# Turning q and k of two batches with DMA transposes instead of TensorE, in a fused attention and FFT-gate kernel, with its schedule planned anew

## The chip, the cores and the metric

The kernel runs on one core of one Trainium2 chip. The metric is the time of one execution on the device in microseconds (us); three runs of the kernel before took 175.73, 176.09 and 177.28 us, median 176.09.

## The reference

Four batches, eight heads, 768 positions, head size 64. Attention sees the first eight keys (global) and the last 96 (local), with a bias for distance. Its output is projected to three parts; the middle one is convolved over the sequence through an FFT, multiplied with the other two, and projected again. Inputs and output are float32.

```python
# attention: q, k, v are (4, 8, 768, 64)
scores = (q @ k.T) / 8 + bias          # -slope * distance, slopes 2**-(h+1)
keep = (pos_k < 8) | ((rel >= 0) & (rel < 96))
a = softmax(where(keep, scores, -1e9))
x = (a @ v)                             # to (4, 768, 512)
# gate
x1, x2, x3 = split(x @ w_proj, 3)       # w_proj is (512, 1536)
conv = irfft(rfft(x2, axis=1) * rfft(filter_fft, axis=0))
out = (x1 * conv * x3) @ w_out          # (4, 768, 512)
```

## The kernel before

**Engines and names.** TensorE (PE) does the matmuls and transposes, ScalarE (ACT) and VectorE (DVE) copy the results from PSUM banks to SBUF and do the elementwise work, GpSimd (POOL) issues the loads, and SyncE (SP) issues the stores and a few small copies. POOL's loads read float32 from HBM and write fp16 into SBUF: they cast on the way.

**Attention, `attention(b)`.** For each batch the rows of q go to `qn` (six tiles of 128 rows), those of k to `kn` and of v to `vn` (seven tiles of 120 rows each, below eight rows that hold the global keys). `qn` and `kn` exist once, so a load of the next batch waits until the tile there was read; `vn` exists twice. A matmul of the scores needs q and k with the head dimension on the partitions. For batches 1 to 3 the method `transposes` does this for one tile: four PE transposes of 128x128, each with two heads, into one PSUM bank (line 938), then one copy on ACT or DVE to `QT` or `KT` (line 567). After k tile 0, a DVE copy spreads the eight global columns in `KT` over all seven tiles. `QT` and `KT` exist once as well. Batch 0 comes in pairs of heads in another layout (`load_pair`, `transpose_pair`, line 630): pair 0 is loaded as float32 by SP and cast by ACT or DVE, pairs 1 to 3 are cast by POOL's loads.

The tiles come in three groups, `GRP = [(0, 1), (2, 3), (4, 5, 6)]`. For each group and each pair of heads `scores` does the matmuls (line 975), ACT the exponentials (line 990), DVE the mask (line 997); `values` does the second matmul (lines 1015 and 1020), DVE divides by the sum (line 1039), and `transpose_x` turns the result into `xT` (line 1060).

**Gate and convolution.** `gate` projects `xT` to the first and third part (line 1098); `butterfly` and `conv(b)` do the middle part: projection (line 1159), forward transform (line 924), products with the filter's spectrum on DVE, inverse transform (lines 1181 and 1184), and in `project` the last matmul (line 1215), a copy to `ot` and the store by SP. The filter's spectrum is made in the kernel too.

**The order.** The program is first written down as a graph of operations (`Plan.op`), each with its engine or choice of engines, a cost in us, what it reads and writes, and the PSUM banks it takes. `lay` then goes through the graph like a list scheduler: among the operations that can start first on their engine, it takes the one with the lowest rank. A rank is the operation's batch and place in it plus a number from the list `NUDGES` (2112 numbers, two for each operation: one for the rank, one for the choice between ACT and DVE). `FAVOUR` is a constant in that choice. DMAs have a cost for the issue, and a cost for each packet on the DMA engines, which SP's and POOL's share. Each engine then runs its list in order. `fill` puts idle matmuls (line 563) where PE would wait long. Attention of batch b+1 is so mixed with the convolution of batch b.

Of the kernel before, what the change touches and what calls it, by code (L numbers as in the profile page):

```python
# [17 lines left out]
NG = 8  # L18
# [46 lines left out]
class Plan:  # L65
# [90 lines left out]
    def lay(self):  # L156
# [84 lines left out]
        830, 19469, 28342, 22698, -36791, 44557, 0, 38863, 17326, 50370, 0, 17086, -14969, 46246, -10719,  # L241
        3803, 22479, 12714, -995, -27474, -4380, 3973, 17122, 3529, 7380, -663, -24781, -3497, 45666, -4551,
        -35801, 10005, 0, 12791, 0, -10379, 0, 45454, 0, -5437, 0, -14061, -19757, -14504, -37905, -18946,
        0, -32477, 0, -19819, 0, 19446, -1510, 8329, 0, 27319, 11852, 7297, -33522, -3329, -24534, -36612,
        -27852, 3113, -7029, -29691, -14381, -3884, 31147, 32034, 41013, 3882, -7384, -6372, -2549, 6629,
        68912, 8963, -61766, 5547, -44599, 12091, 18399, 14042, 6929, -4982, -7955, 13539, -24252, 20179,
        -37287, 999, -15997, -18090, 9312, 22827, 23386, 28496, -25966, 23940, -7783, 39729, 0, 1069, 0,
        12644, 0, -10150, 0, 23681, 0, -18062, 0, -19460, 0, 7837, 0, 430, 0, -3637, 0, 8913, 0, -4969, 0,
        4698, 0, 6387, -28901, -14115, 14320, -44762, 8724, -14864, 46735, -14488, 23611, -14772, -11847,
        6451, -3306, -18377, -60, 4689, 27298, 24083, -497, -18877, 16900, 19934, 37256, 19651, -14734,  # L250
        -9560, 12718, -42257, 27146, 1115, -39200, -14114, 6946, -5667, 16361, -49626, -3804, -7768, -67026,
        -18259, 60927, 21512, -46061, 5299, 29871, 21514, -44548, 5866, -12730, -23878, -15725, 33821,
        20215, -25471, 41707, 6771, 23796, 39844, 27531, -14231, -2302, -5026, 6456, 8053, 1663, -7662,
        -1658, -22536, 10581, -5577, -28542, -40863, -38468, -5794, -5468, 40622, -19008, 14370, 67736,
        -58861, 42786, 25155, -29878, -3418, 3618, 4708, -22659, -28259, -20518, 8701, 6031, -6892, -10351,
        -20996, 26804, 20150, 54288, -13311, 5794, 6136, 52867, -15428, -29665, 25192, 30956, 45334, 21269,
        43306, 2557, -24451, 6157, -1880, -4325, -2390, 7965, -31500, -28218, 18854, 4142, 15094, -27249,
        27912, 43510, -17851, -24582, -28451, 3289, -4573, 52435, 13404, 20792, -24567, 15357, -28602,
        -63577, -4124, -16002, 20822, -14047, -23587, 29959, -35143, 9243, -7310, -76644, -8134, 42347,
        15822, -12242, -3646, -30686, 275, 21750, -36005, 1469, 29713, -50088, -42560, -19350, 23864, 5050,  # L260
        -35144, 35778, -23119, -25177, 16491, -2020, 4380, -36451, -22654, -22150, -20473, 13426, -26733,
        26609, 6268, -22149, 3957, -50217, -3909, -19153, 2810, -3292, 7853, -21492, 32509, 30392, 1058,
        -3422, 15580, -35441, -9203, -35466, 64502, 42951, -19116, -24283, 2677, -62640, -12510, -59703,
        11602, 21513, 35378, 20196, 11922, -1695, 2261, 5554, -11981, 15156, 12890, -23779, -19040, -49831,
        -15466, -43761, 7442, 2473, -11475, -562, -20186, 44257, -33302, -12882, -28759, 38437, 11482, 1330,
        11240, -38355, 17055, 27903, 51476, 19276, 41100, -22953, 19243, -49765, 30962, -35331, 10963,
        42827, 51939, -23434, -11212, 50785, -4094, -27838, -30215, -24532, -12422, 67855, 13805, 3349,
        -31574, -50206, -1578, -23241, 3462, -29661, 8300, 12759, 26155, 16907, 2610, 5092, 33120, -6934,
        14181, -6832, 37905, -14123, 4017, -27020, -20812, 1598, 3482, -15360, 14795, 14629, 485, 23373,
        31416, -26303, 985, -32770, -12960, -31274, -27569, 14995, 28878, -62352, -24591, -25434, -13467,  # L270
        -1753, 33337, -31036, -11856, -18317, -11803, -33535, -27683, -51311, -11621, 1840, -23345, -13880,
        -10610, -21888, -29421, -35794, 9291, 16111, -10016, -61858, 13788, 28430, 11863, 10235, 26016,
        -11573, 27177, -20634, 32822, -31295, 24126, 16224, 34719, 32835, 36139, 40036, 830, 39163, 18794,
        23592, 7759, 51877, 15207, 11097, 5209, -31196, 47785, 18050, 12543, -18408, 3112, 9419, 28821,
        33481, 24315, -4637, -2954, 58662, 10982, 44569, -17852, -13026, 18502, 18480, 661, 39608, 43043,
        5607, -6149, 51251, -23733, 21791, 22094, 13091, 28673, -13130, 38566, 29894, 58869, 14114, 22687,
        13217, 23944, 14851, 18542, 32490, 39556, 0, 2287, 0, 19051, 0, -4358, 0, -11746, 0, 19030, -37967,
        1328, 0, -1449, 14563, -17652, -982, -19950, 0, -1349, 0, -11190, 0, 2329, 0, 1474, 0, 9498, 0,
        18549, 0, 6688, 0, 22215, 0, 20539, 0, 3845, 0, 18493, 0, -9540, 0, 5625, 0, -4323, 0, -8046, -3533,
        -19460, 16225, 5133, -15664, 1868, -10430, 13679, -822, -6032, 46722, 17, -12126, -14344, -697,  # L280
        -13742, -12505, 35119, 19976, 12563, -17553, -4315, -16313, -8060, -26919, -13513, 5645, -9234,
        -8261, 33619, 1834, -2859, -2550, 21273, 8957, -13081, -9314, 20868, 8922, -5132, 5559, 6221,
        -35799, 24500, 3519, -6685, 3949, -816, -6213, 9623, -62952, -17310, 10679, 22559, -35498, 10601,
        -12029, 6157, 5514, 7375, -48803, 10526, -28598, 4222, -27669, -30984, 26626, 10987, -54583, -53116,
        -15825, 15071, -78852, -9661, 6714, 2840, -38629, -19587, -4267, 24678, -95876, 18875, -65326,
        37035, -57223, 2718, -80355, 8544, -25562, 24290, -40863, 2118, -56826, 1618, -8022, -31710, 24818,
        3620, -25827, 27844, -44889, 2870, 4692, 1799, -40217, -9884, -31044, -26859, 10139, -30260, 15490,
        -10550, -33083, -6484, -3536, 42406, -39070, 25617, -4598, 29316, -41708, 15965, 36737, 22936,
        -38817, 8527, -48993, 22443, 17760, 28836, -35248, -5369, -32024, 12970, -29506, 46391, 21693,
        -7287, -24248, -581, -2018, 24139, -49992, 23604, -37246, -19201, -50818, 32705, -650, -7523, -9491,  # L290
        -6925, -30680, 1857, -10661, 4404, 11499, 32387, -17435, -48594, -14949, -4657, -84287, -8566,
        14498, -17867, 2527, 39846, -8706, -27278, 52664, 6571, -35366, -320, -10331, -13919, -41255,
        -14510, -27402, 30994, -7841, -31169, -15489, 10258, -20175, 13543, 2857, 2578, 131, -1314, -20053,
        -3100, 4481, -24160, -39099, 11687, -27948, -9199, -2494, 30419, -9029, -805, -6822, -33325, 13405,
        -16820, -66296, -481, -11964, 10636, -6248, -15247, -30087, 9838, -10144, -26515, -24439, -29855,
        -22320, -23621, -44190, -16823, -1332, 20402, -52166, -32146, 29136, -8657, -32420, -27767, 19595,
        4945, -41783, -6152, 22710, -839, 24762, 12982, -46639, 45086, -32249, -27885, 26993, 32349, -1139,
        -27028, 5428, -35713, -11537, -21816, 4520, 11355, -11306, -17012, 4480, -2042, -15007, 18089,
        16310, 5551, -12842, -12327, -74283, -24015, -51377, 27730, -6713, 30891, -54126, 34332, -19745,
        -18476, -68884, 4160, 17961, -25458, -47047, -23408, -74718, -25716, -25378, 10363, -21807, -25577,  # L300
        -30760, -512, -35125, -15528, 5905, 11983, -39028, 8438, -56403, -744, -68035, -9455, -28679, 15786,
        -55653, 8176, -11569, -5453, 4461, 21051, 30451, 38894, -23961, -22340, -37283, -19384, -14914, 91,
        -24447, -19426, -32077, 21216, 6861, -6808, -6892, 5217, 10775, -14628, 70698, 20491, 17063, -9496,
        43779, -27379, 19441, -35221, 40472, -6558, 6850, 27498, 19585, 24533, 14892, -3738, -53050, 27975,
        -49714, -29727, 2330, -4593, -32440, 10709, 5615, -11179, -8091, 16512, -42979, 22940, -7459,
        -19376, -58359, -5155, 3527, 14869, 75937, 14885, 50802, -44287, 9855, -3550, 31325, 23170, 11445,
# [1108 lines left out]
```

## Time and profile before

| | |
|---|---|
| three runs | 175.73, 176.09, 177.28 us; median 176.09 |
| the profiled execution | 177.28 us, span in the profile 175.5 us |
| granted PE clock, mean over the span | 0.996 of full |
| PE | 166.9 us busy, 95% of the span, 1768 matmuls |
| DVE | 157.0 us, 89% |
| ACT | 152.6 us, 87% |
| POOL | 75.3 us, 43%, all of it before 99 us |
| transposes of whole tiles, line 938 | 156 matmuls, 219 to 220 ns each, first at 38.1 us, last at 111.7 |
| scores of batch 2 | first at about 72 us, last at 104 |
| scores of batch 3 | first at about 117 us, last at 134 |

The span is the profiled execution's time on the engines; its own time has the start and end around it as well. The busy time of PE counts each matmul from start to end; since they are pipelined, one may take 219 ns and the next start after 56. In the lists of groups, a line says which engine ran which operation, what it wrote from what, the shape and the number, then busy time, the mean of one in ns, and how long the engine sat idle just before, with what ended the wait. In the chain, each row is a start, a length and what ran.

### The profile page before, as it was taken

The page shows a single profiled execution, that of the slowest core. Times are in us where ns is not written, and L with a number is a line of the kernel's source. Part 1 is how long each engine was busy: PE and PEld are TensorE (multiplying, and loading weights), DVE is VectorE, ACT ScalarE, POOL GpSimd, SP SyncE. Part 2 cuts the span into 40 slices and gives each one's busy share as a digit, 9 for nine tenths or more (in the row PEclk, how much of TensorE's full clock was granted, in tenths as well). Part 3 has the DMA queues.
Part 4 walks back from the last instruction along what each step waited for, and adds up shares of the span by engine and source line. Part 5 has one row for each costly group of instructions (what it writes and reads, how often), then busy time and mean ns, then how long its engine had stood idle before and what let it go on. Part 6 is the DMA issues. An engine that isn't in the chain of part 4 may idle for free.

```text
span 175.5 us, 4566 instructions
## 1 busy us (share of the span) xinstructions
PE 166.9 (95%) x1768; PEld 104.3 (59%) x1768; DVE 157.0 (89%) x368; ACT 152.6 (87%) x304; POOL 75.3 (43%) x97
## 2 busy tenths in 40 slices
PE   7799999999899799999999999999999999999991
PEld 2357777665457567575446669754556674547540
DVE  6669778999999769999999998999899999998960
ACT  8879989999999778999997977999799897968751
POOL 7999986298997699998040300000000000000000
PEclk9999999999999999999999999999999999999998
DMA  5999999999999999999999900000710000043145
GB/s 177 148 145 134 146 200 209 166 152 138 135 166 159 132 141 142 146 144 149 66 63 344 70 4 4 0 0 0 294 70 4 0 2 4 0 159 140 60 166 197
DMA packets 79853, 20.06 MB, mean 114 GB/s; under 512 B 70528, under 2 KB 76888, under 8 KB 79832
## 3 DMA queue, kind: packets, MB, share of 16 engines
q0 software_dynamic: 75408, 12.47, 107.2%
q1 hardware_dynamic: 4424, 7.30, 11.5%
q8 instruction: 14, 0.23, 0.5%
q14 instruction: 7, 0.06, 0.1%
HBM read 25.69 MB, written 6.29 MB: 182 GB/s over the span
## 4 chain that ended last, share of the span: by engine, by line
PE 64%; DVE 14%; DMA 9%; POOL 5%; ACT 5%; issue 2%; ACTq 0%; POOLq 0%; DVEq 0%
PE bank L1098 19%; PE bank L1215 12%; DMA qn<-in_q_dram 9%; PE bank L1159 6%; PE bank L1181 4%; PE bank L1015 4%; PE bank L924 4%; PE bank L938 3%; PE bank L1020 3%; PE bank L975 3%; PE bank L1060 3%; ACT E L990 3%; POOL kn L583 2%; POOL vn L583 2%; PE bank L630 2%
## 5 line engine op out<-in xcount | busy, mean ns | idle before, releaser
L1098 PE MATMUL bank<-xT,w 128*128 128x384 f16 x256 | 45.6, 326 | 0.0
L990 ACT ACTIVATE E<-bank 128x864 f16<-128x864 f32 x48 | 41.0, 923 | 1.7 <-PE bank L975 1.3
L1098 PEld LDWEIGHTS <-w 128*128 128x128 f16 x256 | 23.9, 98 | 15.8 <-issue 0.8
L583 POOL DMA_DIRECT2D kn<-in_k_dram x24 | 21.6, 908 | 14.0 <-PE bank L938 6.6
L583 POOL DMA_DIRECT2D vn<-in_v_dram x29 | 26.2, 922 | 2.0 <-DMA w<-in_moe_w_proj_dram 1.6
L1215 PE MATMUL bank<-wo,y 128*128 128x512 f16 (+1 forms) x100 | 21.8, 371 | 0.1
L583 POOL DMA_DIRECT2D qn<-in_q_dram x21 | 18.6, 892 | 5.9 <-PE bank L755 3.2
L997 DVE TENSOR_TENSOR E<-E,mask 128x864 f16<-128x864 f16 x36 | 20.9, 597 | 0.1
L1039 DVE TENSOR_TENSOR xn<-bank,rc 128x512 f16<-128x512 f32 (+1 forms) x24 | 18.5, 775 | 0.4
L571 ACT ACTIVATE ot<-bank 128x512 f32<-128x512 f32 (+1 forms) x23 | 13.1, 606 | 5.1 <-PE bank L1215 5.0
L1108 ACT CAST g<-bank 128x384 f16<-128x384 f32 x32 | 15.7, 494 | 1.4 <-PE bank L1098 1.2
L1015 PEld LDWEIGHTS <-E 128*128 128x128 f16 x224 | 14.1, 97 | 3.6 <-DVE E L997 1.1
L571 ACT ACTIVATE ab<-bank 128x512 f16<-128x512 f32 x23 | 14.3, 633 | 2.2 <-PE bank L1159 2.0
L1215 PEld LDWEIGHTS <-y 128*128 128x128 f16 x100 | 9.5, 98 | 10.7 <-DVE y L1257 0.8
L1015 PE MATMUL bank<-vn,E 128*128 128x65 f16 x224 | 15.8, 194 | 0.0
L571 ACT ACTIVATE x<-bank 128x384 f16<-128x384 f32 x28 | 13.8, 507 | 2.3 <-PE bank L1098 1.8
L1020 PE MATMUL bank<-vn,E 128*128 128x65 f16 x192 | 15.4, 193 | 0.0
L975 PE MATMUL bank<-QT,KT 64*128 64x216 f16 (+2 forms) x224 | 15.0, 241 | 0.1
L1020 PEld LDWEIGHTS <-E 128*128 128x128 f16 x192 | 13.3, 97 | 0.4
L567 ACT CAST X<-bank 128x512 f16<-128x512 f32 x21 | 12.3, 643 | 0.0
L975 PEld LDWEIGHTS <-KT 64*128 64x128 f16 x224 | 8.3, 94 | 5.6 <-issue 3.0
L924 PE MATMUL bank<-ab,fwd 128*128 128x512 f16 x40 | 11.4, 379 | 0.0
(144 smaller groups left out, 358.2 us busy)
## 6 DMA issues: line engine op xcount, KB each, us to landing
out_dram<-ot SPq DMA_DIRECT2D x23, 256.0 KB
vn<-in_v_dram POOLq DMA_DIRECT2D x28, 120.0 KB, 6.1
kn<-in_k_dram POOLq DMA_DIRECT2D x21, 120.0 KB, 6.0
qn<-in_q_dram POOLq DMA_DIRECT2D x18, 128.0 KB, 6.7
w<-in_moe_w_proj_dram POOLq DMA_DIRECT2D x4, 256.0 KB, 7.3
g<-in_moe_filter_fft_dram POOLq DMA_DIRECT2D x1, 768.0 KB, 12.5
qn<-in_q_dram POOLq DMA_DIRECT2D x3, 192.0 KB, 5.0
kn<-in_k_dram POOLq DMA_DIRECT2D x3, 192.0 KB, 5.1
```

The lines of the kernel that those rows point to most:

```text
L571: self.nc.scalar.mul(out, in_, c)
L583: return self.g.op(eng, 0.57 + 0.00035 * nbytes[0] if eng == "G" else 0.5, lambda _: e.dma_start(dst, src), w=w, r=r, nbytes=nbytes, name= ...
L924: self.nc.tensor.matmul(b.f32(), self.fwd[:, f], src(i, t), start=(n == 0), stop=(n == len(terms) - 1))
L975: nc.tensor.matmul(bs[hh].f32()[:, off:off + w], self.KT[hs, hp, P * m:P * m + P], self.QT[hs, hp, KL * m:KL * m + w], start=(off == 0 and ...
L990: g.op("A", act(864), lambda _: nc.scalar.activation(eo, bs[0].two()[:, :, 0:432].rearrange("p h (m w) -> p h m w", m=2), Act.Exp, scale=s ...
L997: g.op("V", dve(864, 2), lambda _: nc.vector.tensor_mul(eo, eo, mk), r=[("E", hp, gi), ("mask", hp)], w=[("E", hp, gi)], name="masked")
L1015: nc.tensor.matmul(o[:, n, hh], ef[:, at:at + P], vt[:, t, 2 * hp + hh, :], start=first, stop=(t == 0), skip_group_check=True)
L1020: nc.tensor.matmul(o[:, n, hh], ef[:, at:at + P], vt[:, t - 1, 2 * hp + hh, :], start=False, stop=True, skip_group_check=True)
L1039: nc.vector.tensor_mul(to, o[:, :, :, 0:D], rc.to_broadcast([P, 2, 2 * nt, D]))
L1098: nc.tensor.matmul(bk.f32()[:, 0:h], self.w[:, c, o + P * j:o + P * j + P], self.xT[:, c, h * s:h * s + h], start=(c == 0), stop=(c == 3))
L1108: g.op("A", act(h), lambda _: nc.scalar.copy(x3, pts[1].f32()[:, 0:h]), use=[pts[1]], w=[ko], name="x3")
L1215: nc.tensor.matmul(bk.f32()[:, 0:n], y[:, c, P * t:P * t + P], self.wo[:, c, cs], start=(c == 0), stop=(c == 3))
```

## The change

For batches 2 and 3, all tiles of q and k are turned by a DMA. Where `attention` called `transposes`, it calls `turned`; this looks in the set `CROSS` and, for a tile in it, writes one operation for SP: a DMA transpose from `qn` or `kn` in SBUF to `QT` or `KT` in SBUF, with a planned cost of 1.3 us for the issue and 512 packets for the DMA engines. No PSUM bank, no PE transposes and no copy are used then. Since the DMA writes whole tiles of `KT` with their global columns, the eight global rows of `kn` have to be there first: two small SP copies inside SBUF, from k tile 0 (`load_global`, which did this for `vn` alone and now does it for `kn` too), in place of the DVE copy in `KT`. Each k transpose waits for one of the two.

`FAVOUR` goes from 0.1 to 0, and `NUDGES` is another list of 2064 numbers, so the order of nearly everything, and the choice of ACT or DVE for copies, is planned anew. In the code of the changed kernel the DMA transpose has line 956, and the lines of the old methods move by two to fifteen.

On SP's queue the order is then: the first copies as before; for batch 2 two Q transposes, the two copies in `kn`, a Q transpose, the two copies in `vn`, then ten transposes; one Q transpose of batch 3, five stores of batch 0, the copies in `kn`, two Q transposes, the last store of batch 0, the copies in `vn`, and the ten transposes left; then all other stores. POOL's order of loads is nearly as before; a load of batch 3 into `qn` or `kn` waits for a DMA transpose of batch 2 where it waited for PE.

```diff
     NUDGES = (
-        830, 19469, 28342, 22698, -36791, ...
+        ...
     )
-    FAVOUR = 0.1
+    FAVOUR = 0.0
...
+    CROSS = frozenset((b, w, t) for b in (2, 3) for w in "qk" for t in range(7))
...
             if t == 0:
-                self.load_global(vt, s)
-
-    def load_global(self, vt, s):
+                self.load_global(vt, ("vng", s), ("vn", s, 0), ("vn1", s))
+
+    def load_global(self, tile, key, *r):
         for c, (t, n) in enumerate(((0, 2), (2, 5))):
-            self.load("S", vt[0:NG, t:t + n], vt[NG:2 * NG, 0:1].to_broadcast(
-                [NG, n, self.H, self.D + 1]), [("vng", s, c)], (8 * n, 1040), "vglobal",
-                r=[("vn", s, 0), ("vn1", s)])
+            self.load("S", tile[0:NG, t:t + n], tile[NG:2 * NG, 0:1].to_broadcast(
+                [NG, n, self.H, tile.shape[-1]]), [key + (c,)], (8 * n, 1040), "global", r=r)
...
+    def turned(self, b, what, t, src, cols):
+        if (b, what, t) not in self.CROSS:
+            self.transposes(what, t, src, cols)
+            return
+        dst = (self.QT if what == "q" else self.KT)[:, :, cols:cols + P]
+        keys = [("kng", min(t // 2, 1))] if what == "k" else []
+        self.g.op("S", 1.3, lambda _: self.nc.sync.dma_start_transpose(
+            out=dst, in_=src.rearrange("p h d -> p (h d)")), r=[(what + "n", t)] + keys,
+            w=[(what.upper() + "T", t)], nbytes=(512, 650), name=what + "T")
+        if what == "k" and t == 0:
+            self.g.writer["KTg"] = self.g.writer[("KT", 0)]
...
                 for t in new:
-                    self.transposes("q", t, self.qn[:, t], P * t)
+                    self.turned(b, "q", t, self.qn[:, t], P * t)
                 for t in self.GRP[c]:
-                    self.transposes("k", t, self.kn[:, t], P * t)
+                    self.turned(b, "k", t, self.kn[:, t], P * t)
...
                 self.load_rows(("kn",), self.kn, self.k, b, t)
+                if t == 0 and (b, "k", 0) in self.CROSS:
+                    self.load_global(self.kn, ("kng",), ("kn", 0))
```

## The prediction

> **What bounds the kernel now.** I read the page first: three engines are nearly full, and TensorE (PE) most.
>
> ```profile
> PE 166.9 (95%) x1768; PEld 104.3 (59%) x1768; DVE 157.0 (89%) x368; ACT 152.6 (87%) x304; POOL 75.3 (43%) x97
> DMA  5999999999999999999999900000710000043145
> q0 software_dynamic: 75408, 12.47, 107.2%
> q1 hardware_dynamic: 4424, 7.30, 11.5%
> PE 64%; DVE 14%; DMA 9%; POOL 5%; ACT 5%; issue 2%; ACTq 0%; POOLq 0%; DVEq 0%
> ```
>
> The chain that ended last is PE for 64%, and the DMA engines are full until about 100 us: POOL's loads, which cast to fp16 on the way. The page's row of the granted PE clock is full throughout, so no term changes with it. Then I read the chain in order of time. From 64 to 88 us it runs over DVE; after that, to 171 us, almost only over PE, and the transposes of q and k (line 938) lie on it:
>
> ```profile
> 49.13 9.36 DMA qn<-in_q_dram
> ...
> 109.61 1.12 PE bank L938 x20
> 110.73 0.34 PE bank L1060 x6
> 111.06 0.89 PE bank L938 x16
> ```
>
> Twenty transposes take 1.12 us of the chain, 56 ns each. Last the groups by shape, for the copies behind the transposes, and SP's queue:
>
> ```profile
> L567 ACT COPY KT<-bank 128x480 f16<-128x480 f16 x15 | 8.8, 604 | 0.6 <-PE bank L938 0.6
> L567 ACT COPY QT<-bank 128x512 f16<-128x512 f16 x13 | 8.0, 626 | 0.5 <-PE bank L938 0.5
> L567 DVE COPY KT<-bank 128x480 f16<-128x480 f16 x6 | 2.3, 396 | 0.0
> ```
>
> An ACT copy costs 0.6 us and a DVE copy 0.4 for each transposed tile. SP's queue, in the timeline from 55 to 70 us, issues this and nothing else; it is where the new transposes go:
>
> ```profile
> 60.71 1.42 SPq L583 DMA_DIRECT2D vn<-vn  x2
> ```
>
> **What is removed.** *PE:* batches 2 and 3 have 6 + 7 tiles each, four transposes a tile: 104 x 0.056 = 5.8 us. The new order holds three more idle matmuls in the first 35 us (19 against 16); the first scores stand 1.4 us of PE work later than before (12.5 against 11.1), by the first gates 1.0. I take +0.9, between 0 (they fill a wait) and 1.4. To check, I priced each kind of PE step at the pace it keeps when it does not wait (gate 0.65 us, projection 0.86, inverse 0.33, and so on from the timeline) and added them along both orders: 162.2 us before, 157.4 after, **-4.8**. In the profile the last output step starts at 171.1 us, by pure PE work at 162.5: 8.6 us are waits, 5.4 of them collected by 66 us, 7.0 by 87. I keep these waits.
> *ACT:* its K copies fall from 15 to 5 and its narrow Q copies from 13 to 2: 10 x 0.604 + 11 x 0.626 = 12.9 us. It takes over other copies (two wider Q copies, three eo, two x, two ot); by rows its sum falls by 9.
> *DVE:* four K copies (0.396), two 128x224 copies (0.225) and one Q copy (0.418) go, 2.5 us; the planner also moves copies to ACT, and by rows the sum falls by 7.5.
> So all three full engines lose 5 to 9 us, and PE loses least: -4.8 is the gain if nothing new waits.
>
> **What is added.** 28 transposes on SP's queue, line 956, and two pairs of small copies of the eight global K rows, which SP issues before K transposes. No row shows a crossbar transpose. I call p the pace of one after another, for issue and transfer together, and bound it. One moves 128 KB, by the kernel's plan in 512 pieces, 32 for each of the 16 engines. Least: the loads keep POOL at one per 0.9 us with about 1,000 pieces each, so 0.5 us for 512. From the queue rows, a packet takes 0.115 x 16 x 175.5 / 4424 = 73 ns on q1 and 40 ns on q0: one piece at a time 32 x 73 ns = 2.3 us, and with a load's packet between any two 32 x 113 ns = 3.6 us. So 0.5 to 3.6. The nearest row is SP's own SBUF-to-SBUF copy under the loads: the pair of the last fence was issued from 60.71 us, and its packets ran from 62.3 to 65.7, 3.4 us for two. I take **p = 1.7**.
>
> Now what waits for them. Expected time is pure PE work plus the waits collected by then. Batch 2: its q tile 2 landed at 58.5 (49.13 + 9.36) and its k tile 0 by 60.05, where PE turned it. SP then issues in order two global K copies, the third Q transpose, two global V copies (held until V tile 0, 60.7), and the K transposes from about 64. With 3 us to land (the shortest load of 120 KB took 3.5 in all):
> - first scores need two: 64 + 2p + 3 = 70.4; PE gets there at 66.6 + 5.4 = 72.
> - second group, four more: 64 + 6p + 3 = 77.2; PE 74 + 5.8 = 79.8.
> - third, four more: 64 + 10p + 3 = 84; PE 87 + 7 = 94.
> Batch 3: SP's queue holds its second and third Q transposes behind five output writes of batch 0 and behind the second scores of batch 2, 81 + 6.5 = 87.5. Then 2p, an output and four copies (0.7 each, by the same fence), 2p and 3 us of landing: 94 + 4p = 100.8 against 98 + 7.3 = 105; next 94 + 8p = 107.6 against 108 + 7.6 = 115.6; next 94 + 12p = 114.4 against 118 + 8 = 126. All hidden, with 1.6 us the thinnest cover. From p = 2.13 the second group of batch 2 is late.
> The loads share the DMA engines: 14 transposes of batch 2 at 1.7 us take 24 us of a stretch (60 to 83) in which POOL issued 26 loads without a wait. If all of it is pushed on, POOL's run of loads that ended at 83 us ends at 107, lands 6 later (the page's median) at 113, and the last scores of batch 3 need it by 126 - 3 - p = 121. Cost nothing, under a cover of 8 us; if that is gone, each us late is a us. What PE gains or loses at the six hand-overs lies between -1.0 (its own wait for q tile 2 before 58.54, which now falls to SP) and +1.6 (the thinnest cover used up); I take +0.4, near the middle: **-4.8 + 0.4 = -4.4**.
>
> **A rule against it.** PE's transposes take 219 ns in the groups and follow each other at 56. The Trainium skill, "VectorE: DVE Perf Modes", section on the three transpose paths, gives 1309 ns for a 128x128 tile on the DMA crossbar and prefers TensorE where PSUM will do. Four such tiles make an estimated p of 5.2 us, and by the formula of the first rival the time would be 220 us. No run here shows it.
>
> **The sum.** The profiled execution has a span of 175.5 us and its own time of 177.28, 1.8 outside; that is the slowest of three, median 176.09. Profiled: 177.28 - 4.4 = 172.9. Against the median, 176.09 - 4.4 = **171.7**.
>
> **Rivals.**
> - *The transposes become the bound (slower).* Place: SP's queue, from the second scores of batch 2 on. From p = 2.13 that group is late by 6p - 12.8, and by the last scores of batch 3 the queue is late by 94 + (6p - 12.8) + 12p - 126 = 18p - 44.8 in all. At p = 2.73 the gain is gone; at p = 2.9, 7.4 us late, 176.1 - 4.4 + 7.4 = 179.1; at 3.6, 20 late, 192. For it: the DMA row of nines while batch 2 goes through, and 73 + 40 ns above. Against: 1.7 us for the nearest copy. Chance 0.25.
> - *DVE sets the pace.* It is 89% busy and the chain runs over it from 64 to 88 us. Without what the planner moved to ACT, it loses 2.5 us, and the time is 173.6; with a wait or two more, up to 175. Against: ACT has 9 us of room, so the moved copies find a place. Chance 0.17.
> - *It doesn't do what it says:* the late loads hold batch 3's scores and eat the gain, near 176. The cover of 8 us speaks against it. Chance 0.06.
>
> **How the numbers follow.** The forecast has 0.52: 170.0 to 173.3, the lower end where all of DVE's and PE's savings count (176.1 - 6), the upper with 1.6 us of new waits. The range goes on into the first rival up to p = 2.9: 170 to 179; above and below it lie 0.2. A measurement of this kernel tells about 1% from no change, 174.3 to 177.9. Faster: 0.52 + 0.11 of the DVE case = 0.63; same: 0.06 of that case, 0.04 of the late loads and 0.03 of the first rival = 0.13; slower: 0.22 + 0.02 = 0.24.
>
> **What would show it.** PE near 161 busy and 1,667 matmuls; PE transposes of whole tiles only in batch 1 (52); ACT about 143, DVE about 150. Transposes of line 956 issued from about 55 us, under 2.1 us apart, and no wait of the scores' weight loads on QT or KT over 0.5 us. It is wrong if PE shows waits for DMA before scores at 72 to 80 or 105 to 126 us, if transposes follow each other at more than 2.7 us, or if DVE fills the chain beyond 88 us.

## The result: 4.6% slower, and the profile after

The changed kernel took 184.78 us (median of four, 184.09 to 185.04), the kernel before 176.47 beside it: ratio 1.046 [1.041, 1.052]. Ratios here leave out executions in a slower state of the chip; where they and the medians differ, the ratio is meant. I had forecast 171.7. The removed work did go: the page shows 1667 matmuls for 1768, and DVE and ACT 7 to 8 us less busy.

```profile
PE 162.6 (89%) x1667; PEld 99.3 (54%) x1667; DVE 149.3 (82%) x353; ACT 146.0 (80%) x291; POOL 75.1 (41%) x97
PE   7798999999892039989999999999999999999991
PEclk9999999999999756999999999999999999999999
DMA  6999999999999999999999999651026000024135
q0 software_dynamic: 75408, 12.47, 104.3%
q1 hardware_dynamic: 18712, 10.83, 28.8%
PE 66%; DMA 13%; DVE 8%; POOL 7%; issue 3%; ACT 2%; POOLq 0%; ACTq 0%
```

The loads (q0) are as many packets as before, SP's queue (q1) has 18712 for 4424, and the DMA engines are full to 114 us (25 slices) where they were to 101. In the chain DMA has 13% for 9%. The second to fourth rows are 40 slices of 4.6 us. In slices 13 to 15 PE falls to 2, 0 and 3 tenths, and the granted clock then to 5 and 6 tenths: one hole. The kernel before, in slices of 4.4 us, had none:

```profile
PE   7799999999899799999999999999999999999991
PEclk9999999999999999999999999999999999999998
```

The view of waits names who stood there in the changed kernel:

```profile
DVE rc L1053 <- PE bank L1029: 15.6, 4, 12.1
PE bank L935 <- DMA vn<-in_v_dram: 10.8, 1, 10.8
POOL kn L581 <- PE bank L935: 8.4, 1, 8.4
```

The columns are the sum, the number and the longest. DVE waits for PE, POOL waits for PE, and PE waits at line 935, once, for a DMA. Line 935 is a PE transpose, and PE's timeline shows that it is one of **batch 1**, which the change leaves on PE:

```profile
55.72 0.39 PE L935 MATMUL bank<-ident,qn 128*128 128x128 f16 x4
66.93 0.58 PE L935 MATMUL bank<-ident,kn 128*128 128x128 f16 x4 [10.83 <-DMA vn<-in_v_dram]
```

What does it read? A whole tile of `kn`, the eight global rows on top included. And SP's timeline shows who writes these rows:

```profile
56.05 2.67 SPq L956 DMA_TRANSPOSE QT<-qn  x2
58.83 1.52 SPq L581 DMA_DIRECT2D kn<-kn  x2
60.51 1.54 SPq L956 DMA_TRANSPOSE QT<-qn  x1
62.16 1.45 SPq L581 DMA_DIRECT2D vn<-vn  x2
65.84 3.87 SPq L956 DMA_TRANSPOSE KT<-kn  x3
```

The copies of batch 2's global K rows go into `kn` from 58.83 us. The graph has no edge between them and batch 1's PE transposes of `kn`, whose reads name the tile and not the global rows. So the copies could come first in the written order, and the program, which keeps that order for memory both touch, made the PE transpose wait for the copy: in the changed kernel's instruction list this transpose waits on the semaphore of that copy, and no PE transpose of the kernel before waits on a copy of SP. (The bracket names a V load; a wait on several semaphores is put down to the one that came last by the profile.) The copy in turn needs k tile 0 of batch 2, but that did not hold it: SP issued the pair at 58.83 us, right behind two Q transposes. What took long was the way from there. In the trace's records of SP's packets those of the two Q transposes run from 58.9 to 63.6 us and those of the pair only from 64.1 to 65.4. Everything on PE's queue stood behind that PE transpose, and PE came back slow:

```profile
56.00:67.00 11.00, 0.17 (x4) 0.10 (x3) 1.25 (x3) 0.19 (x1) 6.90 (x8) 0.74 2.27 146
67.00:75.00 8.00, 8.00 (x61) 4.67 (x61) 4.33 (x10) 5.38 (x11) 3.49 (x4) 0.71 1.74 121
```

These are two windows; after the length come PE, PE's weight loads, DVE, ACT, POOL, then the granted clock. PE was busy 0.17 us of 11; in the next 8 us it ran at 0.71, which costs 8 x 0.29 = 2.3 us. Added to pure PE work as in the prediction, which is an estimate, the waits are 3.5 us before the hole, 14.5 after it, 17.7 by 80 us and 20.6 at the end, where before had 8.6.

That is theory A: the missing edge costs some 11 + 2 us, and that would be all, the 8.3 us lost and the 4.4 forecast. Theory B, its rival, says that the transposes themselves land too late. The experiments undo one at a time.

### The profile page after: what moved, and what is told of

It reads as the page before. It is cut to its first block, busy times and chain, and to the rows that moved or that the text cites. A ratio compares the mean times of both kernels' runs of the same rounds, so it can differ in the third digit from the quotient of the medians.

```text
span 183.1 us, 4412 instructions
## 1 busy us (share of the span) xinstructions
PE 162.6 (89%) x1667; PEld 99.3 (54%) x1667; DVE 149.3 (82%) x353; ACT 146.0 (80%) x291; POOL 75.1 (41%) x97
## 3 DMA queue, kind: packets, MB, share of 16 engines
q1 hardware_dynamic: 18712, 10.83, 28.8%
## 4 chain that ended last, share of the span: by engine, by line
PE 66%; DMA 13%; DVE 8%; POOL 7%; issue 3%; ACT 2%; POOLq 0%; ACTq 0%
PE bank L1107 20%; PE bank L1168 11%; PE bank L1224 11%; DMA vn<-in_v_dram 8%; PE bank L921 6%; DMA w<-in_moe_w_proj_dram 5%; PE bank L1190 4%; PE bank L984 3%; PE bank L1069 3%; PE bank L1024 3%; PE bank L1029 2%; POOL kn L581 2%; POOL qn L581 2%; PE bank L935 1%; POOL vn L581 1%
## 5 line engine op out<-in xcount | busy, mean ns | idle before, releaser
L1107 PE MATMUL bank<-xT,w 128*128 128x384 f16 x256 | 44.3, 326 | 0.5 <-DMA w<-in_moe_w_proj_dram 0.4
L581 POOL DMA_DIRECT2D qn<-in_q_dram x21 | 18.5, 888 | 12.6 <-DMA QT<-qn 7.3
L1224 PE MATMUL bank<-wo,y 128*128 128x512 f16 (+1 forms) x100 | 22.3, 371 | 0.0
L1006 DVE TENSOR_TENSOR E<-E,mask 128x864 f16<-128x864 f16 x36 | 20.6, 593 | 0.0
L569 ACT ACTIVATE x<-bank 128x384 f16<-128x384 f32 x30 | 15.5, 517 | 3.0 <-PE bank L1107 2.4
L1053 DVE RECIPROCAL rc<-bank 128x8 f32<-128x8 f32 (+1 forms) x24 | 5.0, 209 | 15.8 <-PE bank L1029 15.6
L569 ACT ACTIVATE ot<-bank 128x512 f32<-128x512 f32 (+1 forms) x25 | 14.4, 608 | 4.3 <-PE bank L1224 3.6
L569 ACT ACTIVATE ab<-bank 128x512 f16<-128x512 f32 x24 | 14.5, 615 | 3.9 <-PE bank L1168 3.9
L1024 PE MATMUL bank<-vn,E 128*128 128x65 f16 x224 | 16.5, 195 | 0.5 <-ACT E L999 0.2
L1024 PEld LDWEIGHTS <-E 128*128 128x128 f16 x224 | 14.6, 99 | 3.7 <-issue 1.1
L1029 PE MATMUL bank<-vn,E 128*128 128x65 f16 x192 | 16.2, 195 | 0.0
L1029 PEld LDWEIGHTS <-E 128*128 128x128 f16 x192 | 13.8, 99 | 1.6 <-issue 1.1
L565 ACT CAST eo<-bank 128x384 f16<-128x384 f32 x28 | 12.1, 513 | 2.4 <-PE bank L1193 2.3
L565 ACT CAST X<-bank 128x512 f16<-128x512 f32 x22 | 12.9, 614 | 0.8 <-PE bank L921 0.7
```

The costliest lines, as they stand in the source:

```text
L565: {"A": nc.scalar.copy, "V": nc.vector.tensor_copy, "G": nc.gpsimd.tensor_copy}[e](out, in_)
L569: self.nc.scalar.mul(out, in_, c)
L581: return self.g.op(eng, 0.57 + 0.00035 * nbytes[0] if eng == "G" else 0.5, lambda _: e.dma_start(dst, src), w=w, r=r, nbytes=nbytes, name= ...
L1006: g.op("V", dve(864, 2), lambda _: nc.vector.tensor_mul(eo, eo, mk), r=[("E", hp, gi), ("mask", hp)], w=[("E", hp, gi)], name="masked")
L1024: nc.tensor.matmul(o[:, n, hh], ef[:, at:at + P], vt[:, t, 2 * hp + hh, :], start=first, stop=(t == 0), skip_group_check=True)
L1029: nc.tensor.matmul(o[:, n, hh], ef[:, at:at + P], vt[:, t - 1, 2 * hp + hh, :], start=False, stop=True, skip_group_check=True)
```

## The experiments

**1. The edge turned round.** In `program`, which writes the order down, the copies of batch 2 come after batch 1's PE transposes of k; each engine keeps its list.

```diff
+        turns = [o for o in out if o.name == "k" and o.eng == "P" and o.batch[0] == 0.0]
         for o in out:
             need[o] = set(o.preds)
+            if o.name == "kglobal" and o.batch[0] == 40.0:
+                need[o].update(turns)
```

> The changed kernel with one dependency turned round and every engine's order kept: the copy of the global rows into k tiles 2 to 6 for batch 2 waits for batch 1's PE transposes of k, where PE's last transposes of batch 1 waited for the copy. Theory A (the wait of PE at 55.9 to 66.9 us, 10.99 us in one piece, and the lower PE clock after it are the whole loss): no PE wait over 2 us between 50 and 70 us, clock full throughout, waits collected by the end near 8 us instead of 20.6, and a time of 171 to 173.5 us. Theory B (the DMA transposes and the loads behind them are late, and PE would wait for them anyhow): the wait moves to the first scores of batch 2 and the time stays at 179 or more. Theory C (the new order is worse by itself): no long wait, but 176 or more.

177.69 us, ratio 1.004 [1.000, 1.009]. The hole is gone, and by the ratios 7.4 of the 8.2 us with it: for the loss, theory A is shown. But the forecast's 4.4 us did not appear, and PE now waits elsewhere. Its timeline, then the chain, then SP's timeline:

```profile
73.62 0.27 PE L987 MATMUL bank<-QT,KT 64*128 64x216 f16 x2 [1.33 <-DMA KT<-kn]
74.97 0.27 PE L987 MATMUL bank<-QT,KT 64*128 64x216 f16 x2 [1.08 <-DMA KT<-kn]
```

```profile
66.86 8.07 DMA KT<-kn
```

```profile
61.25 1.83 SPq L959 DMA_TRANSPOSE QT<-qn  x1
63.19 1.45 SPq L584 DMA_DIRECT2D vn<-vn  x2
65.56 3.94 SPq L959 DMA_TRANSPOSE KT<-kn  x3
```

These are the first scores of batch 2. The second K transpose, issued at 66.86 us, landed 8.07 us later; I had allowed 3. The trace's records of SP's packets, told apart by their sizes, show where the time went: SP's transfers went in the order of issue, those of the third Q transpose from 65.8 to 68.3 us, those of the V copies from 68.3 to 69.7, those of the first K transpose from 70.3 to 72.4, those of the second from 72.4 to 73.7. So 5.5 of the 8.07 us are time before its first packet. From 73 to 78 us the waits grow by 4.4 us, with a dip of the clock to 0.79 (72 to 80 us). By the end they are 12.1 against 8.6 before: +3.5, which with -4.8 of pure PE work gives -1.3; the spans differ by -0.9. (The two profiled executions flatter it: this one, 176.41 us, was the quickest of its ten, and that of the kernel before, 177.28, the slowest of its four.)

**2. Batch 1's k in memory of its own,** so that no copy can touch it (its global rows are cleared on DVE at the start).

```diff
-                    self.turned(b, "k", t, self.kn[:, t], P * t)
+                    self.turned(b, "k", t, (self.kn1 if b == 1 else self.kn)[:, t], P * t)
...
-                self.load_rows(("kn",), self.kn, self.k, b, t)
+                self.load_rows(("kn",), self.kn1 if b == 1 else self.kn, self.k, b, t)
```

> The changed kernel with k of batch 1 in memory of its own (a part of the output buffers that is idle then), orders kept; the eight rows ahead of the global keys in it are cleared on DVE at the start, which costs up to 1 us there. Nothing joins batch 1's PE transposes and the copies of batch 2 any more. Theory A: as in the run with the turned dependency, 171 to 174 us, and POOL's wait of 8.4 us for PE is gone too. Theory B: 179 or more. If this one is slower than the other by over 2 us, the shared rows were not the whole cause.

179.48 us, ratio 1.018 [1.011, 1.025]. The clearing puts the very first scores 1.8 us later (13.9 us against 12.1 in experiment 1), and by 54 us 0.6 of it is left, so the time says little about the edge; the trace says more. No copy waits for PE here, and yet the copies are not earlier than in experiment 1 (59.57 us there), nor the K transposes:

```profile
55.98 3.47 SPq L957 DMA_TRANSPOSE QT<-qn  x2
59.56 1.51 SPq L582 DMA_DIRECT2D kn<-kn  x2
...
67.07 5.27 SPq L957 DMA_TRANSPOSE KT<-kn  x3
```

```profile
60.41 7.97 DMA vn<-in_v_dram
68.39 8.89 DMA KT<-kn
```

SP's queue and the landing, 8.89 us, set the first scores, where PE waits 4.0 us in two pieces, and not the edge.

**3. PE kept warm.** The changed kernel, with 46 idle matmuls ahead of the transpose that waits.

```diff
         def turn(_):
+            self.busy(idle, b)          # 46 for the last k tile of batch 1
             for i in range(4):
```

> The changed kernel with 46 idle matmuls of 512 columns (about 9.9 us of PE) ahead of the transposes of batch 1 that wait; orders kept otherwise. The wait's end is set by the copy, so PE gets on at the same time, but its clock has not dropped. Theory A says the clock cost 67 to 75 us at 0.71 of full, 8 x 0.29 = 2.3 us: 182 to 183 us. If the clock costs nothing there (DVE or ACT the bound), 184.5 to 185.

184.2 us, ratio 1.036 [1.026, 1.045]. The clock stays full over the hole:

```profile
56.00:70.00 14.00, 10.85 (x67) 5.20 (x64) 1.84 (x5) 0.79 (x2) 7.25 (x8) 1.00 3.01 123
```

By the ratios this is 1.8 us under the changed kernel, near theory A's 2.3 for the slow clock, but the two intervals overlap: that the rest, the far larger part, is the wait is sure, the price of the clock is not.

**4. The wait without DMA transposes.** The kernel before, with two copies into `kn` of this kind, of no use there, ahead of the last k transpose of batch 1.

```diff
+            if o.eng == "P" and o.name == "k" and o.batch[0] == 0.0:
+                self.turns = getattr(self, "turns", 0) + 1
+                if self.turns == 7:
+                    for t, m in ((0, 2), (2, 5)):
+                        self.nc.sync.dma_start(self.kn[0:NG, t:t + m], self.kn[NG:2 * NG, 0:1].to_broadcast(
                            [NG, m, self.H, self.D]))
```

> The kernel before with nothing changed but the two copies of the global k rows of batch 2 added, whose result nobody needs, written down ahead of the last PE transposes of k in batch 1, so that these wait for them. No DMA transposes. Theory A: PE stops at about 60 us until the copies have landed, near 66 or 67, the clock drops, and the time goes from 176.3 to between 181 and 185 us. Theory B: the copies are small (56 KB), and it stays within 2 us of the kernel before.

192.48 us, ratio 1.090 [1.082, 1.098]: more than I expected, as SP issued these copies only at 63.05 us, behind those in `vn`. PE's timeline, with the releaser named this time:

```profile
69.33 0.59 PE L938 MATMUL bank<-ident,kn 128*128 128x128 f16 x4 [12.63 <-DMA kn<-kn]
```

Two copies of 56 KB together suffice for the loss; no transpose is needed.

The next four start from experiment 1 and ask where the 4.4 us went.

**5. Each DMA transpose twice,** the second into dead memory.

```diff
+            self.nc.sync.dma_start_transpose(out=spare.bitcast(F16).rearrange("p (a b) -> p a b", a=4),
+                                             in_=src.rearrange("p h d -> p (h d)"))
```

> The kernel with the edge turned round took 177.7 us; its PE waits for K transposes at the first scores of batch 2 (4.4 us of drift from 73 to 78 us, with a clock dip to 0.79), and nowhere later. Here each DMA transpose is issued twice, the second time into memory that is dead by then, so SP issues 26 more at about 1.25 us each. Theory (transposes and loads share the DMA engines and SP's queue, and the first scores of batch 2 stand on the end of that): five doubled transposes ahead of the second K tile of batch 2 are 6 us, of which 2 or 3 fall into SP's own waits; the first scores come 3 to 4 us later, the third group has 17 us more of queue against a cover of some 10; 183 to 190 us. Rival (the transposes are hidden, and what holds the time at 177.7 is DVE, or the order of the plan): 177 to 179.

199.2 us (196.7 to 201.5), above the range that I gave. PE's timeline:

```profile
78.14 0.36 PE L993 MATMUL bank<-QT,KT 64*128 64x216 f16 x2 [7.05 <-DMA KT<-kn]
81.20 0.36 PE L993 MATMUL bank<-QT,KT 64*128 64x216 f16 x2 [2.69 <-DMA KT<-kn]
95.33 1.08 PE L993 MATMUL bank<-QT,KT 64*128 64x216 f16 x10 [3.86 <-DMA QT<-qn]
```

Some 20 us for 26 more: 0.8 us each. Nothing covers them, at the first scores or later.

**6. PE's work put back:** 104 idle matmuls of 128 columns, ahead of the scores of batches 2 and 3.

```diff
+            for _ in range(back):       # 5, 4, 4 by group of tiles
+                nc.tensor.matmul(bs[0].f32()[:, 0:P], self.idle[:, 0:P], self.idle[:, 0:P], start=True, stop=True)
```

> Here the 104 transposes that PE no longer does in batches 2 and 3 are put back as as many idle matmuls of 128 columns, 20, 16 and 16 ahead of the three groups of scores of each batch; no result uses them. If PE sets the pace in most places, they cost 104 x 0.056 = 5.8 us, less what lies in PE's wait at the first scores of batch 2 (20 x 0.056 = 1.1): 182 us. If the missing gain was lost because PE is not what bounds these batches (DVE or ACT is): 178 us. In between tells the share of the removed work that had been worth time.

187.6 us (184.5 to 188.5): even the quickest is 6.8 us over experiment 1, where 104 x 0.056 is 5.8. Not all of it need be PE's work: the profiled execution, 187.65 us, waited 4.7 us for K transposes, that of experiment 1 2.6. Still, PE's removed work is worth about its price; DVE did not take its place as the bound.

**7. ACT's work put back:** a copy behind each exponential of batches 2 and 3.

```diff
+            if back:
+                nc.scalar.copy(self.slope.rearrange("p a b c -> p (a b c)")[:, 0:512], self.idle)
```

> One ACT copy of 128x512 (by its row about 0.6 us) is put behind each exponential of batches 2 and 3: 24 of them, 14 us of ACT work, nearly what the 21 removed copies were (12.9). ACT is 80 per cent busy in the kernel with the edge turned round, with some 7 us free between 80 and 135 us. If ACT is a bound there: 10 us or more, 188 us. If ACT has room and only the way from scores to mask gets longer: 179 to 183. If ACT is wholly off the path: 178.

183.89 us, ratio 1.041 [1.033, 1.049]: 6.4 us over experiment 1 by the ratios, for 24 x 0.657 = 15.8 us of copies. That is between the cases that I wrote down, and the run does not tell ACT's load from the longer way between scores and mask. Work put back costs time on both engines, so taking it away must have been worth something; that it was paid out again as waiting is what I infer.

**8. Fewer loads ahead of the transposes,** and its control. V of batch 2 is loaded for two heads of eight, 5,376 packets less.

```diff
+        n = 2 if (what, b) == (("vn", 0), 2) else 8
-        self.load("G", dst[P - (hi - lo):P, t, :, 0:self.D],
+        self.load("G", dst[P - (hi - lo):P, t, 0:n, 0:self.D],
```

> The kernel with the edge turned round, but the loads of V of batch 2 bring two of the eight heads (the output of batch 2 is then computed with V rows of batch 0). That takes some 5,000 of the packets away from the DMA engines between 53 and 75 us, and POOL's later loads are issued earlier. Theory (the K transposes of batch 2 land late, 8 us after their issue, since they share the DMA engines with the loads): they land in 5 to 6 us, the waits of 4.4 us at the first scores of batch 2 fall under 1.5, the clock keeps full there, and the time is 174 to 175.5 us. Rival (the landing is late by SP's queue and by the copies ahead, not by the loads): the waits stay, 177 to 178.

> The kernel before with the same cut as the run with fewer V rows: the loads of V of batch 2 bring two of eight heads, the rest of its V rows stay those of batch 0. A control. Theory (the 4 us that this cut gave the kernel with the edge turned round came through the K transposes, which landed earlier): the kernel before has no DMA transposes, so 175.5 to 176.5 us, a ratio of 0.995 to 1.0. Rival (fewer packets help any order, by earlier loads of batches 2 and 3): 172.5 to 174 us.

173.50 us, ratio 0.983 [0.975, 0.992]; the kernel before with the same cut 175.74, ratio 0.997 [0.993, 1.000]. By the ratios the cut is worth 3.7 us to the kernel with DMA transposes and 0.6 to the one without. The chain and PE's timeline show where:

```profile
67.31 6.12 DMA KT<-kn
```

```profile
72.61 0.27 PE L988 MATMUL bank<-QT,KT 64*128 64x216 f16 x2 [0.22 <-DMA KT<-kn]
73.47 0.27 PE L988 MATMUL bank<-QT,KT 64*128 64x216 f16 x2 [0.60 <-DMA KT<-kn]
```

The landing is 6.12 us instead of 8.07, the waits 0.8 instead of 2.4. So a good part of the gain is lost on the DMA engines, which the loads fill. Not all of it: against its control with the same cut the kernel with DMA transposes is 2.3 us faster, about half of the forecast's 4.4 (the last output step starts at 167.1 us here, at 169.4 in the control, at 171.1 in the kernel before). Where the other half goes is open.

**9. An order planned for late landings.** The missing edge put into the graph (the PE transposes also read the key of the global rows), and the operations shifted one by one by a search that replays the plan with later landings. The 1032 operations then stand in the order found (`kept`).

```diff
-            [("kz", t)] if what == "k" else []), name=what)
+            [("kz", t), ("kng", min(t // 2, 1))] if what == "k" else []), name=what)
...
-        return self.program(self.fill(self.lay()))
+        return self.program(self.fill(self.kept()))
```

> All of the change, with the missing edge put into the graph, and the operations in another order: found by shifting operations in the written order, with the plan's landing of a DMA transpose 3.5 to 5 us later and that of the small SP copies half as much later than the plan had it. By that plan the end no longer depends on the landing up to 5 us; it is 6.0 us ahead of the kernel before's plan, and the first scores of batch 2 need their K transposes some 5 us after the copies' turn comes. Theory (what the change lost was the hand-overs at K tile 0 and at the first scores of batch 2, and with these covered the removed 5.8 us of PE and 13 us of ACT work are worth what the forecast said): 171 to 173.5 us, ratio 0.97 to 0.985, PE's waits for KT and QT under 1 us in all. Rival (the time is given back at places that the plan does not see: loads that wait for lanes, DVE): 175 to 178 us.

185.17 us, ratio 1.043 [1.040, 1.046]: a miss. The search had also moved POOL's first loads, where the plan's model of them does not hold. From the waits:

```profile
DVE KT L694 <- DMA w<-in_moe_w_proj_dram: 12.1, 1, 12.1
PE bank L1113 <- DVE KT L694: 11.3, 2, 11.1
```

PE's slices 4 and 5 (of 4.6 us) read 0: batch 0's first scores stood behind loads of the weights, by the profile's reading. It tells nothing of batch 2.

**10. The same search for the kernel before,** as a control.

> The kernel before, no DMA transposes, with its own operations shifted by the same search, as long. Its plan ends 1.9 us earlier than it did. It shows what the search alone is worth: if plan and chip agree, 174.5 us; if the list it had was tuned on more than the plan, 176 to 178. The other run's gain over this one is that of the DMA transposes.

174.79 us, ratio 0.993 [0.990, 0.995]: what a search of that length finds without any DMA transpose.

**11 and 12. The search held to the loads' order** and to all that comes ahead of 44 (50) us in the plan.

> All of the change, the missing edge in the graph, and the operations shifted by the same search as in the run before, but with POOL's loads in the order of the changed kernel and everything ahead of 44 us of the plan left as it was. Landings of DMA transposes are planned 3.5 to 5 us later, those of the small SP copies half as much. PE does eight more gate steps of batch 1 (0.65 us each) ahead of the first scores of batch 2, and SP issues the first K transposes of batch 2 ahead of the copies in V. The plan's span is 5.7 us shorter than the plan of the kernel before, 5.8 shorter than that of the changed order with a landing 3.5 us later. Theory (the late hand-over at the first scores of batch 2 was all that the forecast lacked): 171.5 to 174 us, PE's waits for KT and QT under 1 us together, no dip of the clock. Rival (the gain is given back elsewhere, to DVE and ACT, which are nearly full): 175.5 to 178 us with PE's waits for KT gone.

> The same with another search of the same length, in which everything ahead of 50 us of the plan is left as it was; SP issues the copies of K and the Q transposes as in the changed kernel, and the first K transposes ahead of the copies in V. Its plan's span is 0.4 us longer than that of the other order. It tells how much of the result hangs on one found order. Theory: 172 to 174.5 us. Rival: 175.5 to 178.

Medians 176.88 and 177.14 us; ratios 0.989 [0.983, 0.996] and 0.989 [0.983, 0.995], which is about 175 us: neither theory's number, and their executions scatter, from 173.6 to 179.3 us. The profiled ones took 178.08 and 176.52; there is no trace of a quick one. PE's timeline of the one and the chain of the other:

```profile
76.20 0.64 PE L1113 MATMUL bank<-QT,KT 64*128 64x216 f16 x10 [0.66 <-DMA KT<-kn]
85.11 0.57 PE L1113 MATMUL bank<-QT,KT 64*128 64x216 f16 x8 [3.99 <-DMA QT<-qn]
```

```profile
63.64 9.39 DMA kn<-in_k_dram
73.04 10.75 DMA QT<-qn
```

At the first scores the wait is down to 0.66 us, as planned. But the second group now waits 3.99 us for a Q transpose (3.2 us in the second order). In the second order the chain comes to that transpose from a load of k that landed just before its issue, and it took 10.75 us itself. In these two executions one hand-over was covered and the wait came back at the next, while the loads lasted; whether the quick ones waited there too is not shown.

**13. Batch 3 alone,** with a control. Its transposes run from 83.6 to 112 us; POOL's last load is issued at 95. The search and its limits are those of experiment 11.

```diff
-    CROSS = frozenset((b, w, t) for b in (2, 3) for w in "qk" for t in range(7))
+    CROSS = frozenset((3, w, t) for w in "qk" for t in range(7))
```

> Only batch 3 is turned by DMA, batch 2 by PE as before; the list of operations starts from the order of the kernel before, with the DMA transposes in the places of the PE transposes, and is shifted by the same search (landings 3.5 to 5 us later than the plan had them, POOL's loads in their order, everything ahead of 44 us as it was). PE loses 52 x 0.056 = 2.9 us, ACT and DVE half of what they lost. In its plan the end stands 3.4 us ahead of the kernel before's, and does not move for landings up to 5 us later. Theory (the loss is that the transposes of batch 2 share DMA engines that the loads fill until about 100 us, so wherever the first hand-over is covered the wait comes back at the next; batch 3's stand at the end of the loads and have some 10 us of room): no PE wait for KT or QT over 0.5 us, full clock, 172.5 to 174.5 us. Rival (DMA transposes cost elsewhere too, or the gain was the search's): 175.5 us or more.

> A control: the kernel before, with its operations shifted by the same search under the same limits as the run with batch 3 alone. Its plan's end stands 0.75 us ahead. Expected 175 to 176.5 us; what the run with batch 3 alone gains beyond this is the DMA transposes' own.

171.95 us (171.01 to 172.79), ratio **0.972** [0.969, 0.976]; the control 175.05, ratio 0.988 [0.982, 0.994]. The difference of the ratios, 0.016 x 176.9 = 2.8 us (by the two intervals some 1.5 to 4.1), is what 13 DMA transposes are worth here; 52 x 0.056 = 2.9 us of PE work went. Each order is one find of a search, though, and the two searches on the kernel before (0.993 and 0.988) differ by 0.8 us. The page:

```profile
PE 161.5 (95%) x1716; PEld 100.4 (59%) x1716; DVE 153.9 (91%) x360; ACT 148.0 (87%) x298; POOL 74.6 (44%) x97
PE   7799799999999999999999999999999999999990
PEclk9999999999999999999999999999999999999999
```

And the view of the DMAs, with the number of transposes and the us from issue to landing (a median of those that the profile knows, here one of each kind):

```profile
KT<-kn SPq DMA_TRANSPOSE x7, 7.0
QT<-qn SPq DMA_TRANSPOSE x6, 8.5
```

These two land as late as the others, after 7.0 and 8.5 us, but PE shows no wait for `KT` or `QT` at all: the second K tile is issued at 94.81 us and its scores start at 108.06. This order beats both kernels. Against the controls (0.993 and 0.988), the full change of experiments 11 and 12 (0.989) gains little or nothing: what batch 3's transposes bring, batch 2's take away. That last sentence compares kernels with orders of their own, and is an inference. Batch 2 alone was not run, so that 13 transposes do better than 26 by their place, and not by being fewer, is argued and not shown.

## Why the prediction was wrong

**The step that failed: "two pairs of small copies of the eight global K rows, which SP issues before K transposes".** I gave them a place in SP's queue and asked what they delay there. I did not ask what memory they write and who reads it last. Their destination was in `kn`, which batch 1's PE transposes still read. Every number after 56 us was built on PE arriving at 72 us at the first scores; it stood still from 56 to 67. Cost: 7.4 us by experiment 1 (the ratio falls from 1.046 to 1.004). No rival of mine had this mechanism.

**The second step: "64 + 2p + 3 = 70.4", with PE there at 72.** Without the hole (experiment 1) PE was there at 72.3 us, but the second K transpose landed at 74.93: the cover of 1.6 us became a wait, and a wait for a DMA before the scores at 72 to 80 us was my own sign of being wrong. The term that was wrong is the 64. SP issued the first K transpose at 65.56 us, since the copies of global rows landed just before, and its first packet came at 70.3, since the packets of the third Q transpose and of the V copies were still ahead of it on SP's queue. I had taken a transfer as over once SP had issued it. From there the packets of the two took 3.4 us, which is 2p with my p of 1.7, and the landing 1.2 us more, under the 3 that I allowed: 70.3 + 3.4 + 1.2 = 74.9. The whole of it from issue to landing, 8.07 us, is nearer to the median rows of the profile before, 6.0 to 6.7 us for loads of q, k and v, than to the quickest load, on which I went.

**"Cost nothing, under a cover of 8 us"** for the loads that the transposes push on. The loads were pushed on, from issue to landing by a median of 11.4 us for k and 10.9 for q in experiment 1 where the kernel before has 6.0 and 6.7, and at batch 3's end that cost nothing. But I priced the loads only as the ones to wait. Experiment 8 shows the other direction: the loads hold up the transposes, for some 3.1 us net of the control.

**What stays open.** By the ratios, forecast (0.975) and result (1.046) are 12.6 us apart. Experiment 1 gives back 7.4 and experiment 8 another 3.1 net of its control; the remaining 2.1 no run assigns.

**The rivals.** The first, that the transposes become the bound, named the right resource and the wrong quantity. In experiment 1 SP needed 1.2 to 1.3 us to issue one where nothing held it, and the packets of ten in a row, from the first K transpose on, ran from 70.3 to 90.2 us: 2.0 us each, above my 1.7 and still under 2.13. The second group of batch 2, where I had put the loss, did not wait; the first did, since its transposes started late. DVE as the new bound: experiment 6 speaks against it.

The rule of the Trainium skill, "VectorE: DVE Perf Modes", section on the three transpose paths, 1309 ns for a 128x128 tile, would by my estimate have made p 5.2 us and the time 220. The runs show 1.2 to 1.3 us to issue a transpose of four such tiles, and 0.6 to 0.8 us for its packets where the DMA engines are quiet, 1.3 to 3 under the loads. So the figure, taken four times, does not hold here. The same page's advice, in its rules for kernel authors (TensorE where PSUM will do), fits batch 2 as far as experiments 11 and 12 go, and not batch 3.

**What was right.** The price of the removed work, as far as the runs tell: 5.8 us of PE, at least 6.8 when put back, longer waits included; 2.9 by the same rate and 2.8 measured for batch 3 alone, which within its interval may be luck. Also 1667 matmuls and DVE near 150; ACT at 146.0 was forecast at 143. There are 26 transposes, not 28, and 13, not 14, for batch 2.

## To carry to other kernels

For every operation that a change adds, write down which bytes it writes and who still reads them, before asking what it delays on its own queue; a dependence between engines that the planner's graph does not know turns into a wait wherever the written order puts it. Price a DMA by its issue-to-landing row at that place in the profile, not by the shortest one, and count the transfers that stand ahead of it on its queue: they are not over when they are issued. Where the DMA engines are full, work moved to them can bring the wait back at the next hand-over; move only what is due when they have room.

## What the runs showed of the hardware

- A DMA transpose of 128x512 fp16 within SBUF: 512 packets of 256 B, 18 ns each when quiet; SP issues one in 1.2 to 1.3 us. When quiet, the first packet comes 1.2 us after the issue began and all of them take 0.6 to 0.8 us; the shortest landings were 3.7 to 4.4 us after the issue. Under casting loads the packets took 1.3 to 3 us in the changed kernel and in experiment 1, the first came 2.0 to 7.2 us after the issue, and a landing took up to 12.3 us (experiment 11).
- After PE stood still for 11 us, the granted clock averaged 0.71 for the next 8 us of full work; idle matmuls in the gap kept it at 1.00, and the time was 1.8 us shorter, which is within the scatter. The Trainium skill, "TensorE: Matmul & The Clock Gate", in its part on the clock gate, gives half speed after at least one idle window of about 3.4 us and full speed after at least one busy window of that length. Here 8 us at 0.71 is 4.6 us at half speed, which agrees.
- A wait of one instruction stops its whole engine: 10.83 us on PE became 12.1 on DVE and 8.4 on POOL.
